# Four input loads of a fused attention and feed-forward kernel, issued as two transfers each

## The chip, the cores and the metric

The kernel runs on one core of one Trainium2 chip. The metric is the device time of one execution in microseconds, lower is better; the kernel before takes 241.18 us (median of three runs, 241.02 to 241.27). A core has a matrix engine (TensorE, PE in the profile, with PEld for its weight loads), a vector engine (VectorE, DVE), a scalar engine (ScalarE, ACT), a general engine (GpSimd, POOL), and a synchronization engine (SyncE, SP) that here issues transfers and waits. Each of them runs its own list of instructions in order. They wait for each other, and for transfers, on semaphores.

## The reference

Inputs are q, k and v (8 batches, 8 heads, 576 positions, 64 channels, float32) and four weight matrices. The output is 4608 rows of 512 float32.

```python
q_s = softmax(q, axis=-1)          # over the 64 channels of a position
k_s = softmax(k, axis=2)           # over the 576 positions of a channel
kv = einsum('bhsd,bhse->bhde', k_s, v)
x = einsum('bhsd,bhde->bhse', q_s, kv)   # then heads side by side: 4608 x 512
out = ((x @ w1) * (x @ w2)) @ w3 @ w_out
```

## The kernel before, in words

The four weights stay in the core's memory in 16 bits. At the start the kernel multiplies w3 by w_out once (`fold`, steps `w3t`, `w3T`, `pf`, `W3O`), so that each tile needs one product with the result, `W3O`, in place of two.

`attention(b)` makes x for batch b. Half of the heads lie in partitions 0 to 63 and half in 64 to 127; a batch of q, k or v is one tile of 128 partitions x 4 heads x 9 x 64, 1152 KB. For q: maximum (`qmx`), subtraction (`qsub`), exponential (`qexp`), sum (`qsm`), division (`qn`), then a transpose, from batch 2 on by a transposing transfer on SP (`qd`). For k: maximum (`kmx`, line 484 for the later batches, two heads at a time), subtraction (`ksub`), exponential (`kexp`). For v: a cast to 16 bits, two heads at a time (`vc`). PE then makes kv (`kv`, line 544) and x (`xm`, `xt`, line 662), and x is scaled and stored as 16 bits (`xs`, `xts`).

`chunk(c)` makes the feed-forward part of 512 rows of batch c, and of the rows left over from all batches for c = 8: `up` (line 779) multiplies by w2 and by w1, `bs` copies one product, `ab` (line 794) multiplies the two, `down` (line 801; line 816 in the last chunk) multiplies by `W3O`, `os` copies the result to one of four output buffers, and `st` (line 827; `tail`, line 809, in the last chunk) stores it. A `st` step before the last chunk issues two transfers of 128 KB. In the last chunk each step issues one.

The order of all instructions is written out by hand: `ORDER` lists every step, and `Plan.run` emits them in that order. `PICKS` says which engine does a step where there is a choice.

Loads: `LOADS` go through POOL's queue, `HW` and `LATE` (batches 2 to 7, without k 2) through SP's. Tiles of q, k and v exist twice, so a load of batch b waits until batch b - 2 has been read. A load's step carries its name, for instance `("k", 7)`; `load` (line 402) makes it with one `dma_start`.

SP's list is the loads of `HW` and `LATE`, the stores and the transposing transfers, 100 in all: 2 + 17 loads, 64 + 5 stores and 12 transposes. They signal eight semaphores in turn: the first transfer the first semaphore, the ninth the first again. Before a transfer is issued, SP waits until the one eight places ahead in its list, which signals the same semaphore, has landed. The last transfer is the store of the last half of the last rows, and it signals the fourth semaphore.

At the end of the program SP runs nine wait instructions. The first waits for two semaphores of POOL's transfers. The next eight wait for SP's eight semaphores, one each and in the order first to eighth, each together with one other semaphore (POOL's transfers, DVE, ACT). A drain follows them, and then all engines meet at two barriers. In the profile these instructions have the line number of the program's end, L915, and SP's queue is called SPq.

Of the kernel before, what the change touches and what calls it, by code (L numbers as in the profile page):

```python
# [229 lines left out]
def kernel(  # L230
# [11 lines left out]
    nc = tc.nc  # L242
# [9 lines left out]
    HH = H // G  # L252
# [8 lines left out]
    EPS = 1e-9  # L261
    PARTS = [(0, 4), (4, NJ)]
    WOS = 2
    ROWS = [(0, 1), (1, 2), (2, 3), (3, 4), (4, 6), (6, 8)]
    COLS = [(0, 256), (256, 512), (512, 768), (768, 1024)]

# [11 lines left out]
    def p_o():  # L278
        return po_pool.tile([P, C], F32, tag="po", name="po")
# [6 lines left out]
    g_ = nc.gpsimd  # L286
    dve = nc.vector
    st = {}
# [42 lines left out]
    def moves(n, pool=True):  # L331

        return {"ACT": (0.17 + n / 1220.0, False), "DVE": (0.14 + n / 960.0, False)}
# [32 lines left out]
    def side(name):  # L366

        n, i = name[0], name[1]
        if n in ("wo", "w3"):
            if n == "wo":  # L370
                r = slice(i * N_FT // WOS, (i + 1) * N_FT // WOS)
                dst, src = wosb[:, r, :], moe_w_out.rearrange("(p g) c -> p g c", g=N_FT)[:, r, :]
            else:
                r = slice(*ROWS[i])
                dst, src = w316[:, r, :], moe_w3.rearrange("(r p) f -> p r f", p=P)[:, r, :]
            if name in RAW:
                st["cast", name] = dst
                _, a, x = dst.shape
                dst = raw(name).rearrange("p (a x) -> p a x", a=a)
            return dst, src, []  # L380
        if n in ("w1", "w2"):
            dst, src = {"w1": (w1sb, moe_w1), "w2": (w2sb, moe_w2)}[n]
            cols = slice(*COLS[i])
            return dst[:, :, cols], src.rearrange("(c p) f -> p c f", p=P)[:, :, cols], []
        src = {"k": k, "q": q, "v": v}[n]
        dst = vcast[i] if n == "v" and VCAST[i] else inbuf[n][i % 2]
        view = src[i].rearrange("(h g) (p j) d -> (g p) h (j d)", g=G, j=NJ)
        cut = slice(0, NJ * D)
        if len(name) > 2:
            cut = slice(PARTS[name[2]][0] * D, PARTS[name[2]][1] * D)  # L390
        last = [("cast", *x) for x in RAW if home(x)[0] == (n, i)]
        if i >= 2:
            last = {"k": [("kexp", i - 2, p) for p in range(NHP)],
                    "q": [("qexp", i - 2, p) for p in range(len(PARTS))],
                    "v": [("kv", i - 2)] if VCAST[i - 2] else [("vc", i - 2, p) for p in range(NHP)]}[n]
        return dst.rearrange("p h j d -> p h (j d)")[:, :, cut], view[:, :, cut], last

    def load(name, queue, slot, prev, gate):
        dst, src, last = side(name)

        def go():
            st[name] = (nc.sync if queue == "SP" else g_).dma_start(out=dst, in_=src)  # L402
            if gate:
                tc.add_manual_dep(
                    st[name].ins, st[gate].ins.name,
                    mybir.DependencyInfo(mybir.DependencyClass.Sync, mybir.DependencyReason.DATA),
                    reason="load order")

        plan.add(name, queue, 0.5 if queue != "POOL" else 0.55 if name[0] in ("w3", "wo") else 0.78,
                 go, needs=last + [x for x in (slot, gate) if x], after=[prev] if prev else [],  # L410
                 lead=1e3, size=bytes_of(name))

    def bytes_of(name):
        n = 4
        for x in side(name)[0].shape:
            n *= x
        return n
# [18 lines left out]
    def fold(ft):  # L436
# [11 lines left out]
        def mm(h):  # L448
            if not h:
                st["pf", ft] = p_o()  # L450
            for gt in range(h * N_FT // WOS, (h + 1) * N_FT // WOS):
                nc.tensor.matmul(st["pf", ft], lhsT=st["w3T", ft][:, gt, :], rhs=wosb[:, gt, :],  # L452
                                 start=(gt == 0), stop=(gt == N_FT - 1))

        def sc(eng):
            scale(eng, W3O[:, ft, :], st["pf", ft], ISC)

        row = [r for r, (a, b) in enumerate(ROWS) if a <= ft < b][0]
        plan.add(("w3t", ft), "PE", 0.48, tr, needs=wt(("w3", row)) + [("ident",)], takes="pab")
        plan.add(("w3T", ft), {"DVE": (0.69, False), "ACT": (1.02, False)}, 0, ev, needs=[("w3t", ft)],  # L460
                 gives=[("w3t", ft)], takes="w3T")
        for h in range(WOS):
            last = h == WOS - 1
            plan.add(("pf", ft, h), "PE", 1.74 / WOS, lambda h=h: mm(h),
                     needs=[("pf", ft, h - 1) if h else ("w3T", ft)] + wt(("wo", h)),
                     takes=None if h else ring, gives=[("w3T", ft)] if last else [])
        plan.add(("W3O", ft), moves(C), 0, sc, needs=[("pf", ft, WOS - 1)], gives=[("pf", ft, 0)])

# [451 lines left out]
```

## Time and profile before

| | |
|---|---|
| median of three runs | 241.18 us (241.02 to 241.27) |
| profiled execution | 240.52 us |
| its span, first to last instruction | 238.4 us |
| PE busy in the span | 230.7 us (97%) |
| DVE, ACT, POOL busy | 180.0, 120.7, 112.8 us |
| granted TensorE clock | 1.0 |
| moved by transfers | 45.66 MB, mean 192 GB/s |

The profile follows one execution. A row of a timeline has the start in us from the span's start, the length, the engine, the line of the kernel, the operation and what it writes and reads. A row of one line's or tile's instructions has the count, the shortest, median and longest duration in ns, and the first and last start; a line below gives the shortest, median and longest time of its transfers from issue to landing. A row of waits has who waited for whom, the total in us, how often, and the longest. The issue of a transfer is the time that SP spends on it. The transfer itself goes on after that and ends when it lands.

### The profile page before, as it was taken

What the parts mean: (1) busy time and instruction counts of PE and PEld (TensorE: products, weight loads), DVE (VectorE), ACT (ScalarE), POOL (GpSimd) and SP (SyncE); (2) the same over time, 40 slices, a digit from 0 to 9 for tenths busy, and PEclk for the clock granted to TensorE, in tenths of its full rate; (3) what the DMA queues carried; (4) which work ended last, traced back from release to release, by engine and by line L of the source; (5) the groups of instructions that cost most, each with busy time, mean ns of one, the idle gap of its engine ahead of it and who ended that gap; (6) DMA issues with size and microseconds to landing.
All of it is one profiled execution on the core that took longest, in us unless ns stands there. A gap on an engine that the chain in (4) does not pass through costs nothing.

```text
span 238.4 us, 4957 instructions
## 1 busy us (share of the span) xinstructions
PE 230.7 (97%) x1981; PEld 121.1 (51%) x1981; DVE 180.0 (76%) x275; ACT 120.7 (51%) x221; POOL 112.8 (47%) x74
## 2 busy tenths in 40 slices
PE   7899899999999999999999999999999999999994
PEld 2445559865857544444444444444454444444442
DVE  2977998898899989998998899787567444355610
ACT  1436764668768958768824683557323002200021
POOL 8345445479957986997662933328530000000000
PEclk9999999999999999999999999999999999999999
DMA  6999999999989999688988932540077231030143
GB/s 209 215 294 223 322 220 301 261 370 392 389 210 291 403 205 294 243 235 203 327 270 200 306 147 46 77 111 0 0 150 173 62 71 45 0 91 0 44 132 132
DMA packets 37894, 45.66 MB, mean 192 GB/s; under 512 B 15984, under 2 KB 22384, under 8 KB 37872
## 3 DMA queue, kind: packets, MB, share of 16 engines
q1 hardware_dynamic: 30080, 34.22, 49.3%
q0 software_dynamic: 7792, 11.14, 21.3%
q8 instruction: 15, 0.25, 0.4%
q14 instruction: 7, 0.06, 0.1%
HBM read 38.80 MB, written 9.44 MB: 202 GB/s over the span
## 4 chain that ended last, share of the span: by engine, by line
PE 86%; DMA 5%; DVE 3%; POOL 2%; issue 1%; ACT 1%; POOLq 0%; ACTq 0%
PE pab L779 52%; PE po L801 23%; DMA wosb<-in_moe_w_out_dram 5%; PE po L816 3%; PE pkv L544 2%; PE po L452 2%; PE xm L662 1%; DVE k L519 1%; POOL en L614 1%; POOL w L402 1%; PE po L662 1%; DVE kmx L493 1%; ACT ek L527 0%; PE pkv L554 0%; PE qtp L629 0%
## 5 line engine op out<-in xcount | busy, mean ns | idle before, releaser
L779 PE MATMUL pab<-x,w2sb 128*128 128x512 f16 (+1 forms) x320 | 66.0, 337 | 0.1
L779 PE MATMUL pab<-x,w1sb 128*128 128x512 f16 (+1 forms) x320 | 65.9, 336 | 0.0
L794 DVE TENSOR_TENSOR ab<-pab,bsb 128x512 f16<-128x512 f32 x72 | 48.9, 681 | 16.7 <-PE pab L779 15.2
L801 PE MATMUL po<-W3O,ab 128*128 128x512 f16 x256 | 59.5, 379 | 0.0
L779 PEld LDWEIGHTS <-w1sb 128*128 128x128 f16 x352 | 34.4, 98 | 27.9
L779 PEld LDWEIGHTS <-w2sb 128*128 128x128 f16 x352 | 33.4, 98 | 27.0 <-issue 0.7
L323 ACT CAST bsb<-pab 128x512 f16<-128x512 f32 x49 | 28.3, 585 | 36.5 <-PE pab L779 36.2
L801 PEld LDWEIGHTS <-ab 128*128 128x128 f16 x256 | 24.6, 98 | 28.8 <-issue 0.4
L519 POOL TENSOR_TENSOR k<-k,cb 128x1152 f32<-128x1152 f32 x13 | 33.9, 2626 | 8.1 <-DVE km L496 3.5
L582 POOL TENSOR_TENSOR q<-q,qm 128x1280 f32<-128x1280 f32 (+1 forms) x13 | 27.8, 2142 | 20.7 <-DVE qm L577 12.9
L614 POOL TENSOR_TENSOR en<-eq,qr 128x1024 f16<-128x1024 f16 (+1 forms) x14 | 29.2, 2093 | 17.4 <-DVE qr L607 8.0
L323 ACT COPY osb<-po 128x512 f32<-128x512 f32 (+1 forms) x26 | 14.9, 576 | 35.8 <-PE po L801 28.9
L577 DVE TENSOR_REDUCE qm<-q 128x16 f32<-128x1024 f32 (+1 forms) x16 | 21.4, 1340 | 3.5 <-DMA q<-in_q_dram 3.5
L323 DVE COPY osb<-po 128x512 f32<-128x512 f32 (+1 forms) x11 | 7.3, 667 | 20.8 <-PE po L801 13.7
L595 DVE TENSOR_REDUCE qr<-eq 128x16 f32<-128x1024 f16 (+1 forms) x16 | 21.3, 1341 | 0.5 <-ACT eq L590 0.5
L590 ACT ACTIVATE eq<-q 128x1024 f16<-128x1024 f32 (+1 forms) x16 | 18.6, 1163 | 5.6 <-DVE q L582 3.0
L527 ACT ACTIVATE ek<-k 128x1152 f16<-128x1152 f32 x16 | 18.6, 1165 | 3.6 <-POOL k L519 2.4
L323 DVE CAST bsb<-pab 128x512 f16<-128x512 f32 x23 | 15.8, 687 | 2.7 <-PE pab L779 2.2
L484 DVE TENSOR_REDUCE km<-k 128x128 f32<-128x1152 f32 x8 | 16.9, 2138 | 0.0
L452 PE MATMUL po<-wosb,w3T 128*128 128x512 f16 x64 | 15.0, 379 | 0.6 <-DMA wosb<-in_moe_w_out_dram 0.5
L327 ACT ACTIVATE x<-xm 128x512 f16<-128x512 f32 x14 | 7.9, 596 | 5.5 <-PE xm L662 5.4
L350 PE MATMUL po<-zero 128*128 128x512 f16 x25 | 8.4, 509 | 1.6 <-DVE zero L345 1.6
(70 smaller groups left out, 197.9 us busy)
## 6 DMA issues: line engine op xcount, KB each, us to landing
out_dram<-osb SPq DMA_DIRECT2D x66, 128.0 KB, 2.4
q<-in_q_dram SPq DMA_DIRECT2D x6, 1152.0 KB, 6.8
v<-in_v_dram SPq DMA_DIRECT2D x6, 1152.0 KB, 8.5
k<-in_k_dram SPq DMA_DIRECT2D x5, 1152.0 KB, 7.0
k<-in_k_dram POOLq DMA_DIRECT2D x3, 1152.0 KB, 14.6
v<-in_v_dram POOLq DMA_DIRECT2D x2, 576.0 KB, 14.4
w<-in_moe_w_dram POOLq DMA_DIRECT2D x2, 512.0 KB, 12.0
w<-in_moe_w_dram POOLq DMA_DIRECT2D x4, 256.0 KB, 14.0
```

What stands on the lines that cost most here:

```text
L323: return [(nc.scalar.copy if eng == "ACT" else engine[eng].tensor_copy)(out=out, in_=in_)]
L452: nc.tensor.matmul(st["pf", ft], lhsT=st["w3T", ft][:, gt, :], rhs=wosb[:, gt, :], start=(gt == 0), stop=(gt == N_FT - 1))
L519: return [engine[eng].tensor_tensor(out=kb[:, two(hp), :, :], in0=kb[:, two(hp), :, :], in1=st["cb", b][:, two(hp), None, :].broadcast_to( ...
L527: nc.scalar.activation(out=st["ek", b][:, hp, :, :].rearrange("p j (i d) -> p i j d", i=2), in_=kb[:, two(hp), :, :], func=AF.Exp)
L577: dve.tensor_reduce(out=st["qm", b][:, :, j], in_=qb[:, :, j, :], axis=AX.X, op=ALU.max)
L582: return [engine[eng].tensor_tensor(out=qb[:, :, j, :], in0=qb[:, :, j, :], in1=st["qm", b][:, :, j, None].broadcast_to([P, HH, n, D]), op ...
L590: nc.scalar.activation(out=st["eq", b, p], in_=qb[:, :, j, :], func=AF.Exp)
L595: dve.tensor_reduce(out=st["qr", b][:, :, slice(*PARTS[p])], in_=st["eq", b, p], axis=AX.X, op=ALU.add)
L614: return [engine[eng].tensor_tensor(out=st["en", b][:, j, :, :].rearrange("p j h d -> p h j d"), in0=st["eq", b, p], in1=st["qr", b][:, :, ...
L779: nc.tensor.matmul(st["p", one, c, sub, u][:, a * (t1 - t0):(a + 1) * (t1 - t0)], lhsT=w[:, ct, fb * P:(fb + 1) * P], rhs=x()[:, ct, t0:t1 ...
L794: dve.tensor_tensor(out=st["ab", c][:, nf * u:nf * u + nf, t0:t1], in0=cut(st["p", 0, c, sub, u]), in1=cut(st["bsb", c, sub, u]), op=ALU.mult)
L801: nc.tensor.matmul(st["po", c, tb], lhsT=st["ab", c][:, ft, tb * P:(tb + 1) * P], rhs=W3O[:, ft, :], start=(ft == 0), stop=(ft == N_FT - 1))
```

## The change

Four of the loads on SP's queue are issued as two transfers each: v of batch 6, and q, k and v of batch 7. Each transfer moves two of the four heads of every partition, 576 KB, to where they were moved before. The bytes, the length of the contiguous pieces, the order of the steps and all computation stay as they are. SP's list becomes 104 transfers long, and its last one signals the eighth semaphore. From the second transfer of q 7 on, each transfer of SP signals a semaphore one to four places further than before, and waits for the transfer that is now eight places ahead of it.

```diff
     WOS = 2
+    APART = [("v", 6), ("q", 7), ("k", 7), ("v", 7)]
     ROWS = [(0, 1), (1, 2), (2, 3), (3, 4), (4, 6), (6, 8)]
...
         def go():
-            st[name] = (nc.sync if queue == "SP" else g_).dma_start(out=dst, in_=src)
+            n = HH // 2 if name in APART else dst.shape[1]
+            for x in range(0, dst.shape[1], n):
+                st[name] = (nc.sync if queue == "SP" else g_).dma_start(
+                    out=dst[:, x:x + n], in_=src[:, x:x + n])
```

The first reader of half a tile of k or v (two heads) then waits for its own half. The readers of q take all four heads and wait for both halves. With the waits that go with this, ACT and POOL each run one wait instruction more than before, and DVE one less.

## The prediction

> **What bounds the kernel now.** I read the page first, then the sums by stretches of time, then the chain of work that ended last.
>
> ```profile
> span 238.4 us, 4957 instructions
> PE 86%; DMA 5%; DVE 3%; POOL 2%; issue 1%; ACT 1%; POOLq 0%; ACTq 0%
> ```
> ```profile
> 113.00:136.00 23.00, 23.00 (x189) 10.65 (x188) 21.26 (x31) 12.24 (x28) 14.51 (x8) 1.00 0.93 279
> 136.00:186.00 50.00, 50.00 (x395) 23.08 (x394) 39.02 (x61) 24.86 (x45) 19.77 (x10) 1.00 0.41 89
> 186.00:235.10 49.10, 49.04 (x236) 22.80 (x233) 21.18 (x31) 8.19 (x14) 0.00 (x0) 1.00 0.24 62
> 235.10:238.38 3.28, 0.00 (x0) 0.00 (x0) 0.00 (x0) 0.37 (x1) 0.00 (x0) 1.00 0.36 123
> ```
> The columns of the second fence are stretch, length, busy time of PE, PEld, DVE, ACT and POOL with instruction counts, granted clock, DMA share and GB/s. From 113 us, where the first changed load is issued, to 235.10 PE is busy for all but 0.06 us of 122.1, at clock 1.00. So nothing that only makes data arrive earlier can pay there. The DMA share of 0.93 in 113 to 136 says that the changed loads travel in a crowded stretch. The last 3.28 us hold 0.37 us of ACT and nothing else of the compute engines.
>
> ```profile
> 228.12 6.94 PE po L816 x40
> 235.12 0.37 ACT osb L323
> ```
> ```profile
> L809 SPq DMA_DIRECT2D out_dram<-osb x1: 332/332/332, 235.5 to 235.5; - x1
> DMA to landing us min/median/max: 1.7/1.7/1.7
> ```
> ```profile
> SPq L915 <- DMA out_dram<-osb: 1.1, 2, 0.7
> ```
> That is the chain's end, the last store alone, and SP's waits after 234 us. PE ends, ACT copies until 235.49, SP issues the last store at 235.5, it lands 1.7 later, at 237.2, and SP's closing waits run into two of the stores. The span goes on to 238.4: 1.2 us after the last byte, all waits and barriers.
>
> **The change, part by part.** SP runs 100 transfers; place n (from 0) signals semaphore n mod 8, so the last, place 99, signals the fourth. Four more make 104, and the last, place 103, signals the eighth. At the end SP waits for the semaphores in order, first to eighth, one instruction each. Now four waits stand behind the one that the last store ends; after the change none.
>
> ```profile
> L915 SPq EVENT_SEMAPHORE  x5: 28/28/28, 237.2 to 237.5; - x5
> L915 SPq EVENT_SEMAPHORE  x4: 28/28/28, 237.3 to 237.5; - x4
> L915 SPq EVENT_SEMAPHORE  x4: 28/28/28, 237.2 to 237.4; - x4
> L915 SPq DRAIN  x2: 7/7/7, 237.5 to 237.6; - x2
> ```
> These are the closing waits of SP, asked for in the stretches 237.25 to 237.48, 237.27 to 237.48, 237.25 to 237.47 and 237.50 to 237.62. The second stretch loses the first of the five: it ends at 237.26 to 237.27, so it began at 237.23 to 237.24. The third loses the last of the five: it begins at 237.47 to 237.48. Four steps take 0.24 us, 0.06 each, although each is recorded as 28 ns. The wait that the last store ends is the first of these; the four behind it end late for no other reason than their order. They go: minus 4 x 0.06 = 0.24 us, and the drain behind them starts that much earlier. The four waits are not saved work: after the change they stand ahead, in the 1.3 us (235.9, when SP has issued the last store, to 237.2) in which SP waits for the last stores anyway.
>
> The bounds of this term: 4 x 0.028 = 0.11 if only the recorded part goes, and 0.25 by the widest reading of the brackets (237.23 to 237.48). No instruction is added at the end, which excludes a loss there. I take 0.24, since it is read off the very four.
>
> The Trainium skill, "Perfetto Trace Analysis", section "Sequencer-only Instruction (DRAIN, etc)", says that the profiler records such an instruction only from the moment its semaphores are satisfied to the end of its execution, and leaves out fetch, decode and the push behind it. The trace agrees: 28 ns recorded, 60 ns from start to start. By the record alone the sum would be minus 0.11, by the starts minus 0.24.
>
> Now the cost in the middle: four more issues on SP, and each later transfer of SP waits for a different predecessor (always the one eight places ahead).
>
> ```profile
> 113.14 0.37 SPq L402 DMA_DIRECT2D q<-in_q_dram  x1
> 113.57 2.42 SPq L827 DMA_DIRECT2D out_dram<-osb  x4
> 116.03 0.59 SPq L402 DMA_DIRECT2D v<-in_v_dram  x1
> 122.97 3.62 SPq L637 DMA_TRANSPOSE qT<-en  x2
> 126.73 0.61 SPq L402 DMA_DIRECT2D k<-in_k_dram  x1
> 127.39 6.80 SPq L827 DMA_DIRECT2D out_dram<-osb  x8
> 134.23 0.59 SPq L402 DMA_DIRECT2D v<-in_v_dram  x1
> 146.39 3.33 SPq L637 DMA_TRANSPOSE qT<-en  x2
> ```
> An issue takes 0.37 to 0.61 us. The extra ones of q 7 and v 6 (1.2 us) fall into SP's idle time from 116.6 to 122.97, which ends when POOL has the transposes' input; those of k 7 and v 7 into that from 134.8 to 146.39. So no transpose is issued later. In between, stores move by up to 0.6 us.
>
> ```profile
> q<-in_q_dram SPq DMA_DIRECT2D x1, 1152.0 KB, 6.2
> k<-in_k_dram SPq DMA_DIRECT2D x1, 1152.0 KB, 7.0
> DMA to landing us min/median/max: 5.9/6.7/7.5
> SPq L827 <- DMA k<-in_k_dram: 1.4, 1, 1.4
> ```
> ```profile
> 150.42 1.47 DVE L577 TENSOR_REDUCE qm<-q 128x20 f32<-128x1280 f32 x1
> 142.38 1.14 ACT L323 CAST v<-v 128x1152 f16<-128x1152 f32 x1
> 139.46 2.15 DVE L484 TENSOR_REDUCE km<-k 128x128 f32<-128x1152 f32 x1
> 161.36 1.15 POOL L323 CAST v<-v 128x1152 f16<-128x1152 f32 x1
> ```
> The first fence has the times to landing (third line: the two loads of v), and the one long wait for a load; the second the first reader of each: q 7 lands at 119.3 for 150.42, v 6 at 123.5 for 142.38, k 7 at 133.7 for 139.46, v 7 at 140.1 for 161.36. Slack: 31, 18.8, 5.7 and 21 us.
>
> No whole load in halves stands in this stretch. The nearest is batch 0's q, loaded in two parts at the start:
> ```profile
> L402 SPq DMA_DIRECT2D q<-in_q_dram x2: 447/470/492, 0.7 to 1.2; - x2
> DMA to landing us min/median/max: 4.2/4.8/5.4
> ```
> The second part lands at 1.2 + 5.4 = 6.6, so the pair takes 5.9 us from the first issue, against 6.2 to 7.5 for whole loads. The cost of a split thus lies between minus 0.3 (5.9 against 6.2) and plus 1.7 us (the whole time to landing of the last store, paid a second time). I take the 0.6 of one issue at most; any value of it is inside the smallest slack, 5.7. The store that now waits 1.4 us for k 7 becomes a pair of stores that wait for one half each; v 7 behind them lands by about 140.7, 20 us before its reader.
>
> Stores that land later could hold back the copies into the four output buffers. In 112 to 174 us those wait for PE alone:
> ```profile
> ACT osb L323 <- PE po L801: 11.9, 5, 4.0
> DVE osb L323 <- PE po L801: 3.3, 3, 1.9
> ```
> So the middle costs nothing; one wait instruction more on ACT and on POOL and one less on DVE lie off PE's path too.
>
> **The sum.** The profiled execution took 240.52 us, 2.1 more than its span; minus 0.24 gives 240.28. The runs' median of 241.18 stands 0.66 above the profiled execution. I take the same 0.24 off it: 240.94 us, a gain of 0.10%.
>
> **The rivals.** *Slower: a transfer's fixed time is paid in series.* Then each half keeps SP's rings 1.7 us longer (the last store's time to landing, an upper bound), q 7 and v 6 add 3.4 us, and the transposes of batch 5 queue behind them.
> ```profile
> L637 SPq DMA_TRANSPOSE qT<-en x2: 1328/1668/2007, 123.0 to 125.3; - x2
> DMA to landing us min/median/max: 3.4/3.4/3.4
> 131.01 0.41 PE L662 MATMUL po<-qT,kv 64*64 64x512 f16 x4
> L827 SPq DMA_DIRECT2D out_dram<-osb x4: 537/570/592, 174.5 to 176.4; - x4
> DMA to landing us min/median/max: 2.3/2.3/2.5
> ```
> The second transpose now lands at 125.3 + 3.4 = 128.7, and PE multiplies by it at 131.0. From a delay of 2.3 us on PE stands; 3.4 costs 1.1, so 240.94 + 1.1 = 242.0. For it speaks the 0.93 of the DMA share. Against it: four stores (last two lines) issued within 1.9 us land 2.3 to 2.5 us after their own issue, so their fixed times overlap; batch 0's pair says the same.
>
> The Trainium skill, "DMA: Bandwidth & Descriptors", speaks against the change: "Anatomy of one DMA" gives each transfer a fixed 2.0 us or so (measured on the GpSimd path), and "Rules for kernel authors" asks for 1 MiB or more per transfer. Paid in series, two times 2.0 would make the transposes 4.0 late, an estimate of 242.6. The trace disagrees that it is in series: 2.3 to 2.5 for four stores in a row.
>
> *The change does nothing at the end:* another engine comes to the barrier after SP, 241.18. Against it: the closing drains start at 237.5 to 237.6, right behind the four waits, and SP is the one that is still waiting for stores.
>
> *Faster by more:* the 0.66 us between profiled execution and runs may lie in SP's nine closing waits. Four of nine then save 0.29 more: 241.18 - 0.24 - 0.29 = 240.65. Nothing in the trace places the 0.66 there.
>
> **How the numbers follow.** Forecast 0.74, at 240.94, own range 240.75 to 241.25 (the term's 0.11 to 0.25, and the scatter of runs, 241.02 to 241.27). Nothing 0.07, faster by more 0.09, slower 0.10. A measurement tells about 0.2%, 0.48 us, from no change: 240.70 to 241.66. Forecast and nothing lie in it, all but 0.01: same 0.80, faster 0.10, slower 0.10. The range 240.60 to 241.40 takes in all but the slower case.
>
> **What would show it.** In the profile after: the last store ends the last of SP's closing waits, the drain follows within 0.1 us, and span minus last landing falls from 1.2 to about 0.9. PE stays full from 113 to 235.1 and its last matmul ends where it did. Two stores wait for k 7, none for longer than 2 us. I am wrong if PE shows a gap at L662 after 126 us, if km of batch 7 waits for k, or if the drain starts as late as now.

## The result, and the profile after

The changed kernel takes 240.58 us (median of 12 runs, 240.44 to 240.77). The kernel before, run beside it, takes 241.05 us (12 runs, 240.84 to 241.27). The ratio is 0.9982, with a 95% interval of 0.9975 to 0.9989. The gain is about 0.45 us where 0.24 was forecast. It is real, and just small enough to count as no change by the bound of 0.2% that the prediction set. The forecast ratio, 240.94 / 241.18 = 0.9990, lies just outside the interval.

The profiled execution took 240.50 us, 1.9 more than its span; the one before took 240.52, 2.1 more than its span. These two single executions differ by almost nothing although the medians differ by 0.47. The rows show why. First the page's head, with the shares of the chain that ended last. PE carries 86% of it, as before:

```profile
span 238.6 us, 4962 instructions
PE 86%; DMA 7%; POOL 2%; DVE 1%; issue 1%; ACT 1%; ACTq 0%; DVEq 0%; POOLq 0%
```

The busy time by stretches, with the columns of the prediction's second fence:

```profile
113.00:136.00 23.00, 23.00 (x203) 10.63 (x195) 21.27 (x32) 12.24 (x28) 14.52 (x8) 1.00 0.96 294
136.00:186.00 50.00, 50.00 (x395) 23.05 (x394) 38.86 (x61) 25.35 (x45) 20.23 (x10) 1.00 0.41 91
186.00:235.57 49.57, 49.51 (x238) 23.01 (x236) 21.82 (x32) 8.21 (x14) 0.00 (x0) 1.00 0.24 61
235.57:238.59 3.02, 0.00 (x0) 0.00 (x0) 0.00 (x0) 0.37 (x1) 0.00 (x0) 1.00 0.39 134
```

PE is as full as before, 0.06 us idle in 122.57, at clock 1.00. Its last matmul ends at 235.57, 0.47 later than before, and yet the stretch behind it has shrunk from 3.28 to 3.02 us. So the change gave 0.26 at the end, and something earlier took 0.47. The timeline places that at the start of the program. The two rows of PE below are the first of its stretch without gaps and one product in the crowded stretch, of the kernel after:

```profile
77.09 1.03 PE L783 MATMUL pab<-x,w2sb 128*128 128x256 f16 x8
131.48 0.41 PE L666 MATMUL po<-qT,kv 64*64 64x512 f16 x4
```

and the first of these in the kernel before:

```profile
76.62 1.03 PE L779 MATMUL pab<-x,w2sb 128*128 128x256 f16 x8
```

PE is 0.47 late at 77.09, some 36 us before the first changed load is issued. It is 0.47 late at 131.48 (131.01 before) and still 0.47 late at its end. Nothing between 77 and 235 us was gained or lost. Near the start, PE transposes w3 and waits for a weight to land. In the kernel after, all 24 of these products start at 22.77, after a wait of 1.05 us (first fence). In the kernel before, 16 of them had started at 21.88 and only the last 8 waited, for 0.40 (second fence):

```profile
22.77 1.70 PE L444 MATMUL w3t<-ident,w 128*128 128x128 f16 x24 [1.05 <-DMA w<-in_moe_w_dram]
```
```profile
21.88 1.14 PE L440 MATMUL w3t<-ident,w 128*128 128x128 f16 x16
23.42 0.70 PE L440 MATMUL w3t<-ident,w 128*128 128x128 f16 x8 [0.40 <-DMA w<-in_moe_w_dram]
```

The chain of work that ended last runs through this weight in the kernel after (first fence) and not in the kernel before. It comes to the first product `kv` at 29.24 us in the one and at 28.77 in the other (second fence):

```profile
5.62 17.11 DMA w<-in_moe_w_dram
29.24 0.78 PE pkv L548 x72
```
```profile
28.77 0.78 PE pkv L544 x72
```

From there to the end of PE's last matmul it is 206.33 us in both. The profile of before had a quick start. Over the 108 runs of the kernel before that stood beside the experiments, the span goes from 238.2 to 239.4 us with a mean of 238.84; 13 of them took under 240.5 us. The profiled 238.4 is among the short ones. The 238.6 of after is an ordinary one of its own 12 runs (median 238.65).

The end itself, on SP: the last store, and SP's waits after 234.5 us.

```profile
L813 SPq DMA_DIRECT2D out_dram<-osb x1: 332/332/332, 236.0 to 236.0; - x1
DMA to landing us min/median/max: 1.7/1.7/1.7
```
```profile
SPq L919 <- DMA out_dram<-osb: 0.7, 1, 0.7
```

and SP's closing instructions, asked for in 236.30 to 236.80 (the first row) and in 237.68 to 237.85 (the two others):

```profile
L919 SPq EVENT_SEMAPHORE  x7: 27/28/28, 236.4 to 236.7; - x7
L919 SPq DRAIN  x2: 7/7/7, 237.8 to 237.8; - x2
L919 SPq EVENT_SEMAPHORE  x1: 28/28/28, 237.7 to 237.7; - x1
```

SP's waits now run into one store only, for 0.7 us, where it was two for 1.1. Seven waits run from 236.4 to 236.7 and an eighth at 236.9 (between the two stretches, 28 ns), while the last store is still on its way. One is left; the last store ends it at 237.7, and the drain follows at 237.8. From the last landing (237.68) to the end of the span (238.59) is 0.91 us, against 1.16 before. I call this stretch the tail from here on.

The middle: SP's transfers, by their start and the time that SP spends on them, and its longest wait for a load in 112 to 235 us.

```profile
113.61 0.89 SPq L405 DMA_DIRECT2D q<-in_q_dram  x2
114.55 2.48 SPq L831 DMA_DIRECT2D out_dram<-osb  x4
117.07 1.61 SPq L405 DMA_DIRECT2D v<-in_v_dram  x2
123.45 3.96 SPq L641 DMA_TRANSPOSE qT<-en  x2
127.53 1.50 SPq L405 DMA_DIRECT2D k<-in_k_dram  x2
129.08 5.54 SPq L831 DMA_DIRECT2D out_dram<-osb  x8
134.66 1.12 SPq L405 DMA_DIRECT2D v<-in_v_dram  x2
146.86 3.33 SPq L641 DMA_TRANSPOSE qT<-en  x2
```
```profile
SPq L831 <- DMA k<-in_k_dram: 0.5, 1, 0.5
```

The two rows of transposes start 0.48 and 0.47 later than before, which is the shift of the whole stream. The extra issues took 0.5 to 1.0 us each and went into SP's idle time. Inside the first row, though, the second transpose moved by more:

```profile
L641 SPq DMA_TRANSPOSE qT<-en x2: 1322/1922/2523, 123.4 to 126.1; - x2
DMA to landing us min/median/max: 3.4/3.6/3.8
```

It starts at 126.1 where it was 125.3, about 0.3 us beyond the shift, as the issue of the first took 2.5 us in place of 2.0. PE multiplies by it at 131.48 and does not wait. The wait for k 7 fell from 1.4 to 0.5 us.

How long the halves of q, k and v took (the issues with their first and last start, and below each the shortest, median and longest time to landing):

```profile
L405 SPq DMA_DIRECT2D q<-in_q_dram x2: 374/418/461, 113.6 to 114.0; - x2
DMA to landing us min/median/max: 5.0/5.6/6.2
```
```profile
L405 SPq DMA_DIRECT2D k<-in_k_dram x2: 378/508/638, 127.5 to 128.6; - x2
DMA to landing us min/median/max: 5.1/5.3/5.5
```
```profile
L405 SPq DMA_DIRECT2D v<-in_v_dram x4: 490/590/969, 117.1 to 135.3; - x4
DMA to landing us min/median/max: 5.7/6.3/6.9
```

From the first issue to the last landing a pair takes about 6.6 us for q 7 (114.0 + 6.2 - 113.6) and for k 7 (128.6 + 5.5 - 127.5). Whole they took 6.2 and 7.0. The pairs of v 6 and v 7 took 7.5 and 7.1, against 7.5 and 5.9 whole. The first readers come when they came before, 0.47 to 0.48 later with the stream:

```profile
139.94 2.15 DVE L488 TENSOR_REDUCE km<-k 128x128 f32<-128x1152 f32 x1
142.86 1.14 ACT L324 CAST v<-v 128x1152 f16<-128x1152 f32 x1
150.90 1.48 DVE L581 TENSOR_REDUCE qm<-q 128x20 f32<-128x1280 f32 x1
161.83 1.15 POOL L324 CAST v<-v 128x1152 f16<-128x1152 f32 x1
```

So the mechanism that was forecast is there, with its size: 0.25 us at the end, nothing in the middle. But it is only about half of what the runs gained. The other half doesn't lie in the span at all. The runs show it: each has its time and its span, and the time beside the span is 2.12 us in the mean over the 108 runs before (2.06 to 2.19) and 1.92 over the 12 runs after (1.87 to 1.97). The two don't overlap, although a span is on record to 0.1 us only. That is 0.20 us which the prediction didn't have.

### The profile page after: what moved, and what is told of

It reads as the page before. It is cut to its first block, busy times and chain, and to the rows that moved or that the text cites. A ratio compares the mean times of both kernels' runs of the same rounds, so it can differ in the third digit from the quotient of the medians.

```text
span 238.6 us, 4962 instructions
## 1 busy us (share of the span) xinstructions
PE 231.0 (97%) x1981; PEld 121.0 (51%) x1981; DVE 180.0 (75%) x275; ACT 120.8 (51%) x221; POOL 112.8 (47%) x74
## 4 chain that ended last, share of the span: by engine, by line
PE 86%; DMA 7%; POOL 2%; DVE 1%; issue 1%; ACT 1%; ACTq 0%; DVEq 0%; POOLq 0%
PE pab L783 52%; PE po L805 23%; DMA w<-in_moe_w_dram 7%; PE po L820 3%; PE pkv L548 2%; PE po L456 2%; PE xm L666 1%; DVE k L523 1%; POOL w L405 1%; PE po L666 1%; PE w3t L444 1%; ACT ek L531 0%; PE pkv L558 0%; PE qtp L633 0%; POOL wosb L405 0%
```

## The experiments

Two questions: does the closing term follow the number of waits behind the last store's, and where do the 0.20 us beside the span come from? For the second, four theories stood against each other: the halves themselves, the number of SP's transfers, the place of the last transfer among the eight semaphores, and a property of another engine's list. All of the kernels below were timed in rounds with the kernel before, on four chips; on each of these the kernel before has 2.12 us beside its span in the mean. Their edits are told against the changed kernel.

The table has what was measured of all of them. "Waits behind" are SP's closing waits that follow the one which the last store ends. "ACT's list" is the number of instructions in the program for ACT, waits included; each kernel's profile has two fewer. The tail is that of the profiled execution, the time beside the span is the mean over all runs of the kernel.

| kernel | SP's transfers | waits behind | ACT's list | tail us | beside the span us | median us | ratio to before (95%) |
|---|---|---|---|---|---|---|---|
| before | 100 | 4 | 313 | 1.16 | 2.12 | 241.02 | 1 |
| after | 104 | 0 | 314 | 0.91 | 1.92 | 240.58 | 0.9982 (0.9975 to 0.9989) |
| e1_none | 100 | 4 | 313 | 1.17 | 2.10 | 241.00 | 1.0000 (0.9991 to 1.0009) |
| e2_five | 105 | 7 | 314 | 1.34 | 1.91 | 241.24 | 1.0011 (1.0001 to 1.0021) |
| e3_eight | 108 | 4 | 314 | 1.16 | 1.91 | 240.78 | 0.9993 (0.9984 to 1.0001) |
| e4_small | 104 | 0 | 314 | 0.91 | 1.90 | 240.71 | 0.9983 (0.9974 to 0.9991) |
| f1_act | 100 | 4 | 314 | 1.15 | 1.92 | 240.78 | 0.9993 (0.9984 to 1.0001) |
| f2_small2 | 102 | 2 | 314 | 1.04 | 1.92 | 240.70 | 0.9991 (0.9982 to 1.0001) |
| f3_small1 | 101 | 3 | 314 | 1.11 | 1.92 | 240.75 | 0.9990 (0.9981 to 1.0000) |
| f4_earlier | 104 | 0 | 314 | 0.91 | 1.93 | 240.62 | 0.9987 (0.9974 to 0.9999) |
| g1_act2 | 100 | 4 | 315 | 1.17 | 1.78 | 240.76 | 0.9988 (0.9978 to 0.9999) |
| g2_act8 | 100 | 4 | 321 | 1.15 | 1.87 | 240.87 | 0.9995 (0.9983 to 1.0007) |
| g3_act24 | 100 | 4 | 336 | 1.16 | 1.78 | 240.69 | 0.9992 (0.9980 to 1.0005) |
| h1_both | 104 | 0 | 315 | 0.93 | 1.79 | 240.46 | 0.9980 (0.9971 to 0.9989) |

A ratio here is known to about 0.001, a quarter of a microsecond, and that is as large as either part of the gain. The ratios alone can't tell most of these kernels from each other. The tail and the time beside the span can: the one repeats within some 0.02 us, the other within 0.06 or so from run to run.

### The form of the code alone

```diff
-    APART = [("v", 6), ("q", 7), ("k", 7), ("v", 7)]
+    APART = []
```

> No load is split, so SP has 100 transfers again, as the kernel before. It measures what two like kernels differ by. Order theory (only the closing waits behind the last store count, 0.06 us each): four waits behind it, 1.16 us from the last landing to the end of the span, ratio 1.0000. Halves theory (the split loads themselves gain about 0.2 us more, in the stream or before it): also 1.0000. A ratio of 0.9990 or less would say that the 0.47 us measured for the change are partly scatter of the comparison.

Nothing is gained: 1.0000, a tail of 1.17, 2.10 us beside the span. So both parts of the gain come with the four splits, and neither comes from the loop around the load.

### One transfer too many

```diff
-    APART = [("v", 6), ("q", 7), ("k", 7), ("v", 7)]
+    APART = [("k", 6), ("v", 6), ("q", 7), ("k", 7), ("v", 7)]
```

> Five loads split (k 6 beside the four): 105 transfers, the last signals the first semaphore, and seven closing waits stand behind the one that it ends, against four before and none after the change. Order theory: 0.91 + 7 x 0.06 = 1.33 us from the last landing to the end of the span, ratio (241.05 + 0.18) / 241.05 = 1.0007. Halves theory: the same longer end, less 0.2 us or more for the halves, ratio 0.9999 or less.

With 105 transfers the last one signals the first semaphore, and seven waits stand behind the wait that it ends. In the stretch 237.66 to 238.15 of this kernel, from the landing of the last store on, SP runs

```profile
L919 SPq EVENT_SEMAPHORE  x8: 28/28/28, 237.7 to 238.1; - x8
```

The tail is 1.34 us, 0.43 more than after for seven waits, 0.06 each. The closing term thus follows the place of the last transfer in both directions. A fifth split of the same kind makes the kernel slower than the four by more than all that they gained.

The total leaves a rest. Tail and time beside the span make plus 0.18 and minus 0.21 against before, about zero; measured is plus 0.0011, 0.27 us, with a lower end of 0.0001. The median span of its runs is 239.3 us, where that of after with the longer tail would be 238.65 + 0.43 = 239.08. In its profile PE is as full as in the others:

```profile
113.00:136.00 23.00, 23.00 (x203) 10.64 (x192) 21.26 (x32) 12.24 (x28) 14.52 (x8) 1.00 0.93 290
186.00:235.50 49.50, 49.49 (x238) 22.99 (x235) 21.80 (x32) 8.21 (x14) 0.00 (x0) 1.00 0.24 61
```

So its profiled execution, with a span of 239.0 us, doesn't show where 0.2 us of its runs' spans went. The start of the program scatters by more than this, so it may be the start; that is not shown.

### Eight splits

```diff
-    APART = [("v", 6), ("q", 7), ("k", 7), ("v", 7)]
+    APART = [("k", 5), ("v", 5), ("q", 6), ("k", 6), ("v", 6), ("q", 7), ("k", 7), ("v", 7)]
```

> The last eight loads of SP split: 108 transfers, the last signals the fourth semaphore as before, four closing waits behind it. So the halves are there twice over and the order at the end is that of the kernel before. Order theory: 1.16 us from the last landing to the end of the span, ratio 1.0000. Halves theory: at least 0.2 us gained, ratio 0.9992 or less.

With 108 transfers the last signals the fourth semaphore again, as before the change. The tail is back at 1.16 us, and the closing term is gone. The 0.20 beside the span is still there (1.91), and the ratio is 0.9993. Twice as many halves add nothing to it. So the two parts of the gain are separate, and the second doesn't hang on the order of the closing waits.

### Four small transfers in place of the splits

```diff
-    APART = [("v", 6), ("q", 7), ("k", 7), ("v", 7)]
+    APART = []
+    idle = konst.tile([16, 4, D], F32)
...
+            if (c, tb) == (5, 2):
+                for i in range(4):
+                    nc.sync.dma_start(out=idle[:, i, :], in_=q[0, 0, 0:16, :])
```

> No load split; four loads of 4 KB into a tile that nobody reads stand behind a store of batch 5, where SP is idle. 104 transfers, the last signals the eighth semaphore, nothing behind it. So the order at the end is that of the change, without the halves. Order theory: 0.91 us from the last landing to the end of the span, ratio 0.9990, as much as the change itself if the change's other 0.2 us are scatter. Halves theory: 0.9990 here against 0.9982 for the change.

The second edit stands in `store`, a step `st` of chunk 5. No load is split; four transfers of 4 KB that nobody reads bring the count to 104. The result is that of the change: 0.9983, a tail of 0.91, 1.90 us beside the span. As far as the ratios can tell, the halves as such gain nothing and cost nothing.

### One or two small transfers

The loop of the kernel above, with `range(2)` in f2_small2 and `range(1)` in f3_small1.

> Two loads of 4 KB into an unread tile in place of four: 102 transfers, the last signals the sixth semaphore, two closing waits behind it. Order theory: 0.91 + 2 x 0.06 = 1.03 us from the last landing to the end of the span, 0.12 us less than before. With 1.9 us beside the span (ACT's list is one instruction longer here too) the ratio is 0.9986, with 2.1 it is 0.9995.

> One load of 4 KB into an unread tile: 101 transfers, three closing waits behind the last store's. Order theory: 0.91 + 3 x 0.06 = 1.09 us from the last landing to the end of the span. Beside the span 1.9 us if ACT's length decides (ACT has one instruction more), 2.1 if it takes more than one instruction on SP; ratio 0.9989 or 0.9998.

The tails are 1.04 and 1.11 us with two and three waits behind. The series over all kernels is 0.91, 1.04, 1.11, 1.16 and 1.34 us for 0, 2, 3, 4 and 7 waits: 0.06 to 0.07 for each. In f3_small1 the one wait that the last store ends and the three behind it are seen in 237.6 to 238.3:

```profile
L923 SPq EVENT_SEMAPHORE  x4: 28/28/28, 237.9 to 238.1; - x4
L923 SPq DRAIN  x2: 7/10/13, 238.2 to 238.3; - x2
```

The time beside the span is 1.92 in both, near the 1.90 with four. So the number of SP's transfers doesn't set it: 101, 102, 104, 105 and 108 transfers all give 1.90 to 1.93. Nor does the place of the last one, which signals the fifth, sixth, eighth, first and fourth semaphore in these.

### Other loads split

```diff
-    APART = [("v", 6), ("q", 7), ("k", 7), ("v", 7)]
+    APART = [("q", 5), ("k", 5), ("v", 5), ("q", 6)]
```

> Four other loads in halves: q, k and v of batch 5 and q of batch 6. 104 transfers, nothing behind the last store's wait. Order theory: 0.91 us from the last landing to the end of the span and ratio 0.9982, as for the change, since it does not matter which loads are split. If the place of the halves counts, the ratio differs by more than 0.001.

Tail 0.91, 1.93 beside the span, 240.62 us: as the change. Which loads are split makes no difference that could be measured here.

### One copy more on ACT, no transfer more

What the kernels with 1.90 to 1.93 us beside the span have in common is the length of ACT's list: 314, where before and e1_none have 313. With more transfers of SP, one wait instruction more comes onto ACT. The next kernel adds one instruction to ACT and nothing else.

```diff
-    APART = [("v", 6), ("q", 7), ("k", 7), ("v", 7)]
+    APART = []
+    idle = konst.tile([P, 1], F32)
...
+            if (c, tb) == (5, 2):
+                nc.scalar.copy(out=idle, in_=epst)
```

> No load split, 100 transfers; one copy of one column on ACT is added behind a store of batch 5, into a tile that nobody reads. ACT's list is one instruction longer, as it is after the change, and SP's is as before. All programs so far with 104 or more transfers also had one instruction more on ACT, and took 1.9 us beside the span, the others 2.1. Theory that ACT's length sets the time beside the span: 1.9 us here, ratio 0.9991. Theory that SP's list (or its number of transfers) sets it: 2.1 us, ratio 1.0000. The closing waits are those of the kernel before in both: 1.16 us from the last landing to the end of the span.

SP's list is as before the change, and so is the end. From the landing of the last store on (stretch 237.6 to 238.1), the wait that it ends and four behind it:

```profile
L922 SPq EVENT_SEMAPHORE  x5: 28/28/28, 237.7 to 237.9; - x5
L922 SPq DRAIN  x2: 7/7/7, 238.0 to 238.1; - x2
```

The tail is 1.15 us. But the time beside the span is 1.92, and the median is 240.78 where before has 241.02. The added instruction took 0.20 us of it away. The ratio's interval reaches to 1.0001; the time beside the span, 1.86 to 1.98 in 11 runs against 2.06 to 2.19, leaves no doubt of this part. The page's head has one instruction more than the 4957 of the kernel before:

```profile
span 238.8 us, 4958 instructions
```

The length of the whole program is not what counts. f3_small1 and g1_act2 both have 4959 instructions there, with 1.92 and 1.78 us beside the span; e4_small and h1_both both have 4963, with 1.90 and 1.79.

### More copies on ACT

The same edit with two, eight and twenty-four copies: `(c, tb) in ((5, 2), (5, 3))`, `c in (5, 6)`, and `for _ in range(2 if c > 4 else 0)`.

> Two copies of one column on ACT, none of SP's transfers changed. ACT's list is then 315 instructions long; it was 313 in the kernel before, where 2.1 us lie beside the span, and 314 in every program with 1.9. If 313 is one past the end of something that repeats every two instructions (odd against even), 2.1 us here. If the list has to be longer than a mark, or the step repeats in larger pieces, 1.9. The end of the span is that of the kernel before, 1.16 us from the last landing.

> Eight copies of one column on ACT, behind the stores of batches 5 and 6: 321 instructions on ACT's list, eight more than before. If what repeats is four or eight instructions, 2.1 us beside the span; if it is a mark that 314 passes, or a larger piece, 1.9.

> Copies of one column on ACT behind each store of batches 5 to 7, two each: 336 instructions on ACT's list, 23 more than before. A mark at 314: 1.9 us beside the span. A piece of 16 instructions does not come back at 23 more, so this run only shows whether 1.9 holds further on or other values occur.

Beside the span lie 1.78, 1.87 and 1.78 us with 315, 321 and 336 instructions. So it isn't one step from 313 to 314, nor a matter of odd and even (315 and 321 differ by 0.09, 313 and 315 by 0.34), nor of a remainder by 2, 4 or 8 (313 and 321 agree in all three and differ by 0.25). It doesn't fall steadily with the length either. Two copies were expected to give 2.1 or 1.9, and gave neither. What it is stays open.

It is also not shown that all of it comes off the time of a run. Against the 240.98 us of the kernel before in the same rounds, the medians of the three are lower by 0.22, 0.11 and 0.29 us, where the time beside the span is shorter by 0.34, 0.25 and 0.34. The difference is smaller than the quarter of a microsecond to which a ratio is known.

### Both parts together

```diff
     APART = [("v", 6), ("q", 7), ("k", 7), ("v", 7)]
+    idle = konst.tile([P, 1], F32)
...
+            if (c, tb) == (5, 2):
+                nc.scalar.copy(out=idle, in_=epst)
```

> The change as it is (four loads in halves, 104 transfers, nothing behind the last store's wait) and one copy of one column on ACT behind a store of batch 5, so that ACT's list has 315 instructions, the length with 1.78 us beside the span. If the two parts of the gain are independent: 0.91 us from the last landing to the end of the span, 1.78 beside it, 0.14 us less than the change, ratio 0.9976. If the time beside the span depends on more than ACT's length, 1.9 and ratio 0.9982.

Tail 0.93, beside the span 1.79 (1.74 to 1.83), 240.46 us, ratio 0.9980 (0.9971 to 0.9989). This kernel has the end of the change and the 315 instructions of g1_act2, and it shows both terms at once. Its end, in 237.60 to 237.95:

```profile
L922 SPq DRAIN  x2: 7/10/13, 237.8 to 237.8; - x2
L922 SPq EVENT_SEMAPHORE  x1: 28/28/28, 237.7 to 237.7; - x1
```

It has the lowest median of all kernels, 0.12 us under that of the change. That the two differ is carried by the time beside the span (1.79 against 1.92), not by the ratios.

## Why the prediction was right, and where it fell short

*The closing term was right.* Four steps of 0.06 us, minus 0.24, stood in the sum. Measured are 0.25 between the tails and 0.26 between the last stretches of the two profiles. The series of 0, 2, 3, 4 and 7 waits gives 0.06 to 0.07 for each. The choice between the recorded 28 ns (0.11 in all) and the starts (0.24) was the one point of judgement in it, and the starts were right. The Trainium skill, "Perfetto Trace Analysis", section "Sequencer-only Instruction (DRAIN, etc)", says that the record leaves out fetch, decode and the push. The trace agrees, with 0.06 us saved for a record of 0.028.

*The middle was right.* The product at L666 moved by 0.47 us with the whole stream, not by more; km of batch 7 doesn't wait; the copies into the output buffers wait for PE alone, as before:

```profile
ACT osb L324 <- PE po L805: 11.9, 5, 4.0
DVE osb L324 <- PE po L805: 3.3, 3, 1.9
```

Two details were off. One store waits for k 7, not two, and for 0.5 us. And "no transpose is issued later" does not hold for the second one of batch 5, which is issued about 0.3 us beyond the stream's shift; its slack took that up.

*The step that failed* is the sum: "240.52 us, 2.1 more than its span; minus 0.24 gives 240.28", and ahead of it "one wait instruction more on ACT and on POOL and one less on DVE lie off PE's path too". The first carries the 2.1 us beside the span over as a constant, the second costs the wait on ACT at nothing. PE's path and the span indeed don't show it. But with 314 instructions on ACT the time beside the span is 1.92 in place of 2.12, and f1_act makes that difference with one ACT instruction alone. The missing term is minus 0.20. With it the sum reads 0.25 + 0.20 = 0.45 us; the ratio of 0.9982 is 0.43 of 241.05.

*The number.* The measured 240.58 us lies below the forecast's own range, 240.75 to 241.25, and 0.02 below the wide one, 240.60 to 241.40. On the prediction's base of 241.18 the ratio of 0.9982 would give 240.75, just at the lower end. That "no change" came true is in part luck: the gain was nearly twice the forecast, and 0.18% is only just inside the bound of 0.2%.

*The base.* The 0.66 us between the profiled execution and the median of the runs was taken as the same for both kernels. Most of it was the quick start of the profiled execution, in which PE's stream began 0.47 earlier than in the profile after. To subtract the term from the median was sound; to compare the two profiled executions directly (240.52 and 240.50) would have shown no gain. Whether quick starts are wholly apart from the change is not shown. With the tail taken off each span, 24 of the 108 runs of the kernel before and 3 of the 11 of e1_none lie at 237.4 us or less, where the median is 237.7, but only 4 of the 127 runs of the kernels with a longer ACT list, and none of the 12 of the change.

*The rivals.* "Faster by more" forecast 240.65 and came nearer to 240.58 than the forecast did, but by a cause that isn't there: e3_eight has the closing waits of before and keeps the 0.20, and the change's own span is no shorter than its tail explains (medians of 238.65 and 238.9 us). "The change does nothing at the end" fell with the tail of 0.91. "A transfer's fixed time is paid in series" fell with the transposes: the later one of batch 5 moved by 0.8 us, 0.47 of it with the stream, and not by 3.4. The Trainium skill, "DMA: Bandwidth & Descriptors", "Anatomy of one DMA" and "Rules for kernel authors", speaks for few and large transfers. Here loads of 1152 KB in two halves landed 6.6 to 7.5 us after their first issue, against 5.9 to 7.5 for whole ones. The largest loss of one load is 1.2 us (v 7), less than the forecast's upper end of 1.7, and its reader came 20 us later.

## What to carry to other kernels

A program that ends with one wait for each semaphore should let its last transfer signal the semaphore that is waited for last; count the transfers modulo the number of semaphores, since one transfer more or less moves the end by up to 0.43 us (tails of 0.91 and 1.34 here). The time of a run has a part that the span doesn't show, and it is not a constant: set the run's time minus its span beside the medians before an effect of some tenths of a microsecond is put down to a row of the trace. And before two profiles are compared at their ends, see where their gapless streams begin: here a shift of 0.47 us from the first 77 us hid a gain of 0.26 in the last three.

## What the runs showed of the hardware that was not expected

The time beside the span goes with the length of ACT's list: 2.10 to 2.12 us with 313 instructions (two kernels), 1.90 to 1.93 with 314 (eight kernels with different transfers), 1.78 and 1.79 with 315 (two), 1.87 with 321 and 1.78 with 336 (one each). It doesn't matter whether the instruction that was added is a wait or a copy. No row of a profile shows this time, since it lies outside the span. Whether it is spent ahead of the first instruction or behind the last, and why the length of a list enters into it, was not found out; the lists of SP (172 to 180 instructions) and POOL (116 to 119) varied among the kernels with 1.90 to 1.93 without showing in it, and no engine's list but ACT's was lengthened by itself. Quick starts are rarer with more than 313 instructions too (4 of 127 runs against 27 of 119); that was not expected either, and its cause is open.
